# ScalarE's first activation is an exponential of one zero, issued before the first rows of q and k arrive

## The chip, the cores and the metric

The kernel runs on one core of one Trainium2 chip. The metric is the device time of one execution in microseconds, the median of several runs. Five engines work side by side, each on its own stream of instructions in order: PE (TensorE), DVE (VectorE), ACT (ScalarE), POOL (GpSimd) and SP (SyncE, which here only issues DMAs). They wait for one another through semaphores.

## What is computed

Windowed attention with sink tokens, then a two-layer feed-forward network with a gate h * sigmoid(h), all in float32:

```python
scores = (1/sqrt(D)) * q @ k.T                     # B=4, H=8, S=768, D=64
keep   = is_sink | in_window                       # n_sink=4, window=128: integers given at run time
a      = softmax(where(keep, scores, -1e9))
x      = (a @ v) laid out as (3072, 512)
h      = x @ w_in                                  # 512 x 2048
out    = (h / (1 + exp(-h))) @ w_out               # 2048 x 512
```

The two weights arrive as 64-bit numbers and are turned into float32 on the chip.

## The kernel before

**Tiles and stages.** The 3072 rows are eight chunks of 384 (index c). Each chunk has four pairs of heads, so there are 32 pairs p. Pairs 0 to 7 (chunks 0 and 1) take a path of their own, the functions whose names begin with f_: q and k are transposed by PE against the identity matrix (f_prep, L667), scores are made per head j of the pair (f_scores, L699), the exponential and the division by its sum follow (f_softmax, L737), the probabilities are transposed (f_ptrans, L757) and multiplied with v (f_av, L778). Pairs 8 to 31 take other functions (q_prep, k_prep, v_prep, scores, softmax, ptrans, strans, av). For every chunk, 16 column blocks of h are then made by mlp1 (L843, names h), gated by act (L857, names gh and gl) and multiplied with w_out by mlp2 (L869, names out).

**The weights** come in 32 pieces of 512 KB in four groups (weight, L808): SP loads a piece into the tile wraw, of which there are two buffers, three DVE instructions build the float32 bits in wcv (L41, L42, L43), ACT makes the high part (L826: winh or wouth) and POOL or DVE the low part (L828). A third piece can be loaded only when the L43 of the first is done.

**The masks.** Their limits are the two run-time integers. ACT issues two small DMAs into the tile words (L211), DVE turns them into limits (L215 to L220) and builds the masks m0, m1, m2 and mf (L250 to L276), in order and ahead of everything else that it does. The first instruction of the attention on DVE is L688, which puts the sink keys behind a block of keys kT; the third score matmul of a head reads them. L727 then adds a mask to the scores and takes the row minimum of the negated sum, which the exponential of ACT at L742 uses.

**ACT's first data work** is the copy of transposed q (qlf or qdf, L687) and of transposed k (kT, L684) out of PSUM. ACT holds one table of functions at a time, and an ACT_TABLE_LOAD is placed by the compiler before the first activation that needs another table. In the kernel before the first one stands in front of the first L687 copy, and the copies and the exponentials L742 after it need no other. The gate (Silu, L863 and L864) needs another table, and so the loads alternate later.

**What sets the order.** The program calls the pieces in an order of due times (the table OPT, L928 to L998), and the framework's scheduler then gives each engine its stream: it goes by its own estimates of durations, so a change of one instruction can move others far away. Tiles in pools with one or two buffers make a DMA wait until the last reader of the old contents is done; SP is in order, and a DMA that waits holds everything behind it.

The lines at the head of the program are these:

```python
    ident = const.tile([P, P], F32, name="ident")          # L203
    make_identity(nc, ident)
    warm = OPT["warm"]                                      # L206
    words = const.tile([P, 4], I32, name="words")
    for i, src in enumerate((n_sink, window)):
        nc.scalar.dma_start(words[:, 2 * i : 2 * i + 2], src.bitcast(I32).partition_broadcast(P))   # L211
```

Of the kernel before, what the change touches and what calls it, by code (L numbers as in the profile page):

```python
# [8 lines left out]
F32 = mybir.dt.float32  # L9
F32R = mybir.dt.float32r  # L10
I32 = mybir.dt.int32
AF = mybir.ActivationFunctionType
# [157 lines left out]
def attn_moe_kernel(  # L170
# [11 lines left out]
    nc = tc.nc  # L182
# [19 lines left out]
    const = ctx.enter_context(tc.tile_pool(name="const", bufs=1))  # L202
    ident = const.tile([P, P], F32, name="ident")  # L203
    make_identity(nc, ident)

    warm = OPT["warm"]  # L206

# [827 lines left out]
```

## Time and profile before

| what | value |
|---|---|
| three runs | 722.54, 724.70, 723.37 us |
| their median | 723.37 us |
| the profiled execution's own time | 723.66 us |
| its span in the trace | 721.8 us |
| granted clock of PE over the span | 0.998 |
| PE busy | 705.0 us, 3842 matmuls |
| ACT busy | 489.4 us |
| DVE busy | 481.3 us |
| POOL busy | 281.5 us |
| bytes moved | 61.86 MB |

The profiled execution's time is 1.86 us above its span. A row of the trace gives the start in microseconds from the span's start, the busy time, the engine, the line, the operation, out<-in, and in brackets the idle time ahead of it with what ended it. SPq and ACTq are DMA issues by SP and ACT; the landing of a DMA has no row of its own, and is seen where an engine waits for it. A row with a count above 1 merges instructions of one line.

### The profile page before, as it was taken

How to read it: one execution, taken by the hardware profiler on the slowest of the kernel's cores; microseconds unless marked ns; L12 is line 12 of the kernel's file. 1: busy time of each engine (PE TensorE's matmuls, PEld its weight loads, DVE VectorE, ACT ScalarE, POOL GpSimd, SP SyncE). 2: the span in 40 equal slices, each digit the busy share in tenths (PEclk: the TensorE clock that was granted, in tenths of full speed). 3: DMA queues.
4: the chain of work that ended last, by engine and by line, in shares of the span. 5: the costliest groups of instructions: out<-in, count | busy, mean ns of one | idle time of the engine just before them, and what ended most of it. 6: DMA issues, size and time to landing. Idle time of an engine off the chain costs nothing.

```text
span 721.8 us, 12275 instructions
## 1 busy us (share of the span) xinstructions
PE 705.0 (98%) x3842; PEld 624.1 (86%) x3842; DVE 481.3 (67%) x1323; ACT 489.4 (68%) x1165; POOL 281.5 (39%) x667
## 2 busy tenths in 40 slices
PE   6998999999999999999999999999999999999997
PEld 4676778798999999999999999999999999998986
DVE  5899767976776687667866777767866776731111
ACT  4889788786776777777666777777667876732112
POOL 3310000055655666444555455544554554430000
PEclk9999999999999999999999999999999999999999
DMA  7556546434522262114521353114412321001001
GB/s 180 176 154 186 148 112 173 151 84 107 147 43 40 70 187 63 22 39 138 138 41 27 84 166 66 35 34 120 136 27 41 106 58 35 1 1 45 0 1 46
DMA packets 141334, 61.86 MB, mean 86 GB/s; under 512 B 130001, under 2 KB 130001, under 8 KB 141265
## 3 DMA queue, kind: packets, MB, share of 16 engines
q1 hardware_dynamic: 140976, 61.04, 32.9%
q8 instruction: 31, 0.51, 0.3%
q14 instruction: 39, 0.31, 0.1%
q10 hardware_dynamic: 288, 0.00, 0.0%
HBM read 54.72 MB, written 6.29 MB: 85 GB/s over the span
## 4 chain that ended last, share of the span: by engine, by line
PE 81%; DMA 5%; DVE 5%; ACT 3%; POOL 2%; issue 2%; SPq 1%; DVEq 0%; POOLq 0%; ACTq 0%
PE h L852 32%; PE out L880 11%; PE out L879 11%; PE out L878 11%; PE o L575 4%; DMA wraw<-in_moe_w_in_dram 3%; PE o L788 2%; PE s L468 2%; PE s L464 2%; PE pt L520 2%; DMA wraw<-in_moe_w_out_dram 2%; PE o L591 1%; DVE wcv L43 1%; DVE wcv L42 1%; PE o L584 1%
## 5 line engine op out<-in xcount | busy, mean ns | idle before, releaser
L852 PE MATMUL h<-xh,winh 128*128 128x384 f32 x512 | 177.2, 346 | 0.0
L852 PE MATMUL h<-xh,winl 128*128 128x384 f32 x512 | 173.9, 340 | 0.0
L852 PE MATMUL h<-xl,winh 128*128 128x384 f32 x512 | 172.7, 337 | 0.0
L878 PE MATMUL out<-wouth,gh 128*128 128x512 f32 x384 | 153.2, 401 | 1.7 <-ACT gh L863 1.6
L879 PE MATMUL out<-woutl,gh 128*128 128x512 f32 x384 | 151.8, 396 | 0.5 <-DVE woutl L828 0.3
L880 PE MATMUL out<-wouth,gl 128*128 128x512 f32 x384 | 150.2, 396 | 0.0
L863 ACT ACTIVATE gh<-h 128x384 fp32r<-128x384 f32 x128 | 62.9, 492 | 104.4 <-PE h L852 100.7
L866 DVE TENSOR_TENSOR gl<-sg,gh 128x384 fp32r<-128x384 f32 x128 | 75.4, 589 | 87.2 <-ACT sg L864 84.9
L852 PEld LDWEIGHTS h<-xh,winh 128*128 128x128 f32 x512 | 96.3, 188 | 3.0 <-issue 0.9
L852 PEld LDWEIGHTS h<-xl,winh 128*128 128x128 f32 x512 | 96.5, 189 | 2.1
L852 PEld LDWEIGHTS h<-xh,winl 128*128 128x128 f32 x512 | 96.2, 188 | 0.5 <-issue 0.3
L880 PEld LDWEIGHTS out<-wouth,gl 128*128 128x128 f32 x384 | 71.8, 188 | 17.2 <-DVE gl L866 0.6
L878 PEld LDWEIGHTS out<-wouth,gh 128*128 128x128 f32 x384 | 72.2, 188 | 14.4 <-ACT gh L863 2.4
L879 PEld LDWEIGHTS out<-woutl,gh 128*128 128x128 f32 x384 | 72.1, 188 | 13.2 <-DVE woutl L828 1.3
L505 POOL TENSOR_SCALAR pm<-pm,r 128x128 f32<-128x128 f32 x144 | 61.5, 442 | 42.5 <-DVE r L490 39.2
L485 ACT ACTIVATE pm<-pm,mx 128x264 f32<-128x264 f32 (+1 forms) x144 | 70.6, 492 | 1.3 <-DVE mx L472 0.3
L440 POOL TENSOR_TENSOR vs<-vn,vs 128x256 fp32r<-128x256 f32 (+1 forms) x48 | 33.3, 695 | 91.4 <-ACT vs L438 78.2
L864 ACT ACTIVATE sg<-h 128x384 f32<-128x384 f32 x128 | 62.5, 488 | 0.5
L472 DVE CUSTOM_DVE_ANT_0 pm<-s,m 128x264 f32<-128x264 f32 (+1 forms) x144 | 52.9, 411 | 11.9 <-PE s L468 11.6
L600 DVE TENSOR_TENSOR x<-o,x 64x512 f32<-64x512 f32 x48 | 32.8, 683 | 35.5 <-ACT x L599 34.4
L419 POOL CAST ks<-ksA 128x24 fp32r<-128x24 f32 (+1 forms) x24 | 4.8, 201 | 131.7 <-PE s L468 73.0
L438 ACT CAST vs<-vn 128x256 fp32r<-128x256 f32 (+1 forms) x48 | 18.6, 388 | 50.1 <-PE o L584 49.6
(162 smaller groups left out, 1337.7 us busy)
## 6 DMA issues: line engine op xcount, KB each, us to landing
wraw<-in_moe_w_in_dram SPq DMA_DIRECT2D x16, 512.0 KB
wraw<-in_moe_w_out_dram SPq DMA_DIRECT2D x16, 512.0 KB
wchk<-in_moe_w_in_dram SPq DMA_DIRECT2D x16, 512.0 KB
wchk<-in_moe_w_out_dram SPq DMA_DIRECT2D x16, 512.0 KB
qn<-in_q_dram SPq DMA_DIRECT2D x96, 48.0 KB
kn<-in_k_dram SPq DMA_DIRECT2D x64, 64.0 KB
vn<-in_v_dram SPq DMA_DIRECT2D x32, 128.0 KB
out_dram<-ost SPq DMA_DIRECT2D x7, 512.0 KB
```

Of the source, the lines that this page charges most:

```text
L440: nc.gpsimd.tensor_tensor(vs[:, j0:, j, 1, :], vn[:, j0:, j, :], vs[:, j0:, j, 0, :], ALU.subtract)
L472: nc.vector.tensor_tensor_reduce(out=pm[:, t, off:], in0=sp[:, :w], in1=(m0, m1, m2)[min(blk, 2)], scale=-0.125, scalar=3.0e38, op0=ALU.ad ...
L485: nc.scalar.activation(x, x, AF.Exp, bias=mx[:, p, j * NTB + t : j * NTB + t + 1], scale=-1.0, accum_out=r[:, t : t + 1],)
L505: nc.gpsimd.tensor_scalar(x, x, r[:, t : t + 1], 1.0, ALU.mult, ALU.mult)
L600: nc.vector.tensor_tensor(x32[:, :n], o[0:64, :n], x32[:, :n], ALU.add)
L852: nc.tensor.matmul(hps[:, :CT], w[g][:, cc, fs], s[x], start=n == 0, stop=n == 3 * NCC - 1)
L863: nc.scalar.activation(gh, hps[:, :CT], AF.Silu)
L864: nc.scalar.activation(sg, hps[:, :CT], AF.Silu)
L866: eng.tensor_tensor(gl, sg, gh, ALU.subtract)
L878: nc.tensor.matmul(o, gh[:, ts_], wout_h[g][:, f], start=fc == 0, stop=False)
L879: nc.tensor.matmul(o, gh[:, ts_], wout_l[g][:, f], start=False, stop=False)
L880: nc.tensor.matmul(o, gl[:, ts_], wout_h[g][:, f], start=False, stop=fc == NFC - 1)
```

## The change

A tile of one element is set to zero by DVE, and ACT takes its exponential, in the program ahead of the two small DMAs of the limits. Nothing reads the result.

```diff
     ident = const.tile([P, P], F32, name="ident")
     make_identity(nc, ident)
 
+
+    early = const.tile([1, 1], F32, name="early")
+    nc.vector.memset(early, 0.0)
+    nc.scalar.activation(early, early, AF.Exp)
+
     warm = OPT["warm"]
```

Behind this place every line number of the changed kernel is 5 higher (L687 becomes L692). Numbers at the end of a tile's name are buffer numbers; they are 3 higher in the changed kernel.

**The start of ACT's stream.** Before:

```order
L211 DMA words<-in_n_sink_dram 128x2
L211 DMA words<-in_window_dram 128x2
L687 ACT_TABLE_LOAD
L687 COPY qlf<-qt_173 64x384
L684 COPY kT_181<-kt_174 128x3x128
```

and now:

```order
L216 DMA words<-in_n_sink_dram 128x2
L209 ACT_TABLE_LOAD
L209 ACTIVATE early<-early 1x1
L216 DMA words<-in_window_dram 128x2
L692 COPY qlf<-qt_176 64x384
L689 COPY kT_184<-kt_177 128x3x128
```

The first table load moves from the first copy to the place between the two small DMAs, and the new activation stands behind it. The number of table loads is the same in both streams, 67 (64 of them run in the trace of before; the others stand in a path for other inputs).

**DVE from the third weight piece on** (pairs 0 and 1 of the heads). Before:

```order
L42 SCALAR_TENSOR_TENSOR wcv_2_398<-wraw_2_396,wcv_2_398 128x512
L746 TENSOR_SCALAR r_0_293<-r_0_293 128x3
L43 SCALAR_TENSOR_TENSOR wcv_2_398<-wraw_2_396,wcv_2_398 128x512
L688 COPY kT_280<-kt_273 128x8
L747 RECIPROCAL r_0_293<-r_0_293 128x3
L774 COPY pTz_151<-pb_1_303 128x384
L772 COPY pTz_151<-pa_0_302 8x128
L727 ISA pm_1_0_316,mx<-s_1_0_319,m_94 128x128
```

and now:

```order
L751 TENSOR_SCALAR r_0_296<-r_0_296 128x3
L42 SCALAR_TENSOR_TENSOR wcv_2_401<-wraw_2_399,wcv_2_401 128x512
L752 RECIPROCAL r_0_296<-r_0_296 128x3
L693 COPY kT_283<-kt_276 128x8
L779 COPY pTz_154<-pb_1_306 128x384
L732 ISA pm_1_0_319,mx<-s_1_0_322,m_97 128x128
...
L732 ISA pm_1_2_321,mx<-s_1_2_323,m_99 128x264
L732 ISA mx 128x1
L777 COPY pTz_154<-pa_0_305 8x128
L43 SCALAR_TENSOR_TENSOR wcv_2_401<-wraw_2_399,wcv_2_401 128x512
```

The small copy of transposed probabilities (L772, now L777) has moved behind the three score instructions of the next head, and the third step of the weight piece (L43) behind both. On ACT, at the same place, the three multiplications by the reciprocal (L753, now L758) have moved ahead of the copy L771 (now L776) that the small copy waits for.

**SP around the fifth weight piece.** Before:

```order
L802 DMA wraw_3_443<-in_moe_w_in_dram 128x1024
L642 DMA qn_543<-in_q_dram 128x3x64 x2
L642 DMA kn_544<-in_k_dram 128x3x64
L805 DMA wraw_4_486<-in_moe_w_out_dram 128x1024
L654 DMA vn_313<-in_v_dram 128x3x64 x2
L642 DMA kn_544<-in_k_dram 128x3x64
```

and now:

```order
L807 DMA wraw_3_446<-in_moe_w_in_dram 128x1024
L387 DMA vsn<-in_v_dram 8x4x64
L647 DMA qn_546<-in_q_dram 128x3x64 x2
L647 DMA kn_547<-in_k_dram 128x3x64 x2
L659 DMA vn_316<-in_v_dram 128x3x64 x2
L810 DMA wraw_4_489<-in_moe_w_out_dram 128x1024
```

The fifth weight piece, wraw_4, has moved behind the two loads of vn, into whose buffer pair 0's second product with v must first have been read out.

**ACT at the first gate** (names gh_0 and sg_0). Before:

```order
L753 ACTIVATE pm_0_637<-pm_0_637,r_0_688 128x264
L863 ACT_TABLE_LOAD
L863 ACTIVATE gh_0_698<-h_0_675 128x384
L864 ACTIVATE sg_0_697<-h_0_675 128x384
L826 CAST winh_135<-wcv_2_669 128x512
```

and now:

```order
L868 ACT_TABLE_LOAD
L868 ACTIVATE gh_0_701<-h_0_678 128x384
L758 ACTIVATE pm_0_640<-pm_0_640,r_0_691 128x128
L758 ACTIVATE pm_0_640<-pm_0_640,r_0_691 128x256
L758 ACTIVATE pm_0_640<-pm_0_640,r_0_691 128x264
L831 CAST winh_138<-wcv_2_672 128x512
L869 ACTIVATE sg_0_700<-h_0_678 128x384
```

The load and the first gate have moved ahead of the three multiplications, and the second use of the gate behind them. The streams differ at many more places up to about the 600th of PE's 3944 rows, and PE's order is the same behind that.

## Rows read from the trace of the kernel before

**Rows 1.** The page's head: the span, the busy time of PE, and PE's busy share in 40 equal slices of the span, in tenths.

```profile
span 721.8 us, 12275 instructions
PE 705.0 (98%) x3842; PEld 624.1 (86%) x3842; DVE 481.3 (67%) x1323; ACT 489.4 (68%) x1165; POOL 281.5 (39%) x667
PE   6998999999999999999999999999999999999997
```

**Rows 2.** Stretches of the span (us): its length, then busy us of PE, PEld (weight loads), DVE, ACT and POOL with the number of instructions, PE's granted clock, share of the DMA engines, GB/s.

```profile
0.00:10.00 10.00, 5.91 (x24) 4.55 (x24) 4.61 (x23) 2.60 (x4) 4.12 (x15) 0.93 0.67 142
40.00:50.00 10.00, 10.00 (x55) 6.95 (x54) 8.59 (x26) 8.01 (x23) 1.28 (x1) 1.00 0.60 175
60.00:70.00 10.00, 8.91 (x46) 7.01 (x45) 8.94 (x20) 9.93 (x24) 0.00 (x0) 1.00 0.49 156
200.00:300.00 100.00, 100.00 (x566) 91.92 (x566) 73.12 (x192) 72.29 (x171) 57.14 (x129) 1.00 0.32 76
```

**Rows 3.** ACT in order of time from the span's start: the second of its two DMA issues, the first table load and the first two copies.

```profile
1.35 0.45 ACTq L211 DMA_DIRECT2D words<-in_window_dram  x1
6.20 1.28 ACT L687 ACT_TABLE_LOAD   x1 [6.20 <-PE qt L673]
7.49 0.47 ACT L687 COPY qlf<-qt 64x384 f32<-64x384 f32 x1
7.87 0.47 ACT L684 COPY kT<-kt 128x384 f32<-128x384 f32 x1
```

**Rows 4.** DVE in order of time: its first instruction, the first that reads the limits, the copy of the sink keys, the first mask on scores, and the first step on the second weight piece.

```profile
0.97 0.06 DVE L920 MEMSET one<- 128x1 f32 x1 [0.97 <-PEq L1019]
5.10 0.17 DVE L215 CAST wf<-words 128x4 f32<-128x4 int32 x1 [4.07 <-DMA words<-in_window_dram]
9.83 0.16 DVE L688 COPY kT<-kt 128x8 f32<-128x8 f32 x1
10.08 0.29 DVE L727 CUSTOM_DVE_ANT_0 pm<-s,m 128x128 f32<-128x128 f32 x1
13.23 0.43 DVE L41 TENSOR_SCALAR wcv<-wraw 128x512 int32<-128x512 int32 x1 [0.99 <-DMA wraw<-in_moe_w_in_dram]
```

**Rows 5.** PE and its weight loads in order of time: the first score matmuls, and the weight load of the first third score.

```profile
8.48 2.81 PE L720 MATMUL s<-kT,qlf 128*128 128x128 f32 x6 [1.49 <-ACT kT L684]
10.04 0.50 PEld L720 LDWEIGHTS s<-kT,qlf 128*128 128x128 f32 x2 [0.72 <-DVE kT L688]
```

**Rows 6.** PE in order of time from 20 to 80 us: all rows ahead of which it idled.

```profile
24.18 1.51 PE L788 MATMUL o<-pTz,vn 128*64 128x384 f32 x6 [0.27 <-DVE pTz L772]
28.51 1.51 PE L788 MATMUL o<-pTz,vn 128*64 128x384 f32 x6 [0.46 <-DVE pTz L772]
36.67 1.51 PE L788 MATMUL o<-pTz,vn 128*64 128x384 f32 x6 [0.60 <-DVE pTz L772]
55.77 0.33 PE L765 MATMUL pa<-ident,pm 128*128 128x128 f32 x1 [0.61 <-ACT pm L753]
58.38 0.50 PE L878 MATMUL out<-wouth,gh 128*128 128x512 f32 x1 [0.46 <-ACT gh L863]
64.38 0.50 PE L878 MATMUL out<-wouth,gh 128*128 128x512 f32 x1 [1.09 <-ACT gh L863]
78.89 0.92 PE L720 MATMUL s<-kT,qdf 128*128 128x128 f32 x4 [0.48 <-ACT pTz L776]
```

**Rows 7.** ACT and DVE in order of time around pair 0's second head and pair 1: the copy and the three multiplications on ACT; on DVE the copies of transposed probabilities and the first score instruction of the next head.

```profile
23.23 0.37 ACT L771 COPY pTz<-pa 128x256 f32<-128x256 f32 x1
24.02 1.21 ACT L753 ACTIVATE pm<-pm,r 128x128 f32<-128x128 f32 x3
...
23.41 0.53 DVE L774 COPY pTz<-pb 128x384 f32<-128x384 f32 x1
23.86 0.27 DVE L772 COPY pTz<-pa 8x128 f32<-8x128 f32 x1
24.06 0.27 DVE L727 CUSTOM_DVE_ANT_0 pm<-s,m 128x128 f32<-128x128 f32 x1
24.96 0.07 DVE L727 DVE_READ_ACCUMULATOR2_ANT mx<- 128x1 f32 x1
```

**Rows 8.** SP in order of time: the issue of wraw_4 and of pair 2's vn.

```profile
24.29 0.42 SPq L805 DMA_DIRECT2D wraw<-in_moe_w_out_dram  x1
25.72 0.90 SPq L654 DMA_DIRECT2D vn<-in_v_dram  x2
```

**Rows 9.** DVE and ACT in order of time: the first step on wraw_4, the third step on wraw_3, the reciprocal of pair 2's first head, and the multiplications that read it.

```profile
29.33 0.41 DVE L41 TENSOR_SCALAR wcv<-wraw 128x512 int32<-128x512 int32 x1
29.67 0.69 DVE L43 SCALAR_TENSOR_TENSOR wcv<-wraw,wcv 128x512 int32<-128x512 int32 x1
31.67 0.17 DVE L747 RECIPROCAL r<-r 128x3 f32<-128x3 f32 x1
32.69 1.21 ACT L753 ACTIVATE pm<-pm,r 128x128 f32<-128x128 f32 x3
```

**Rows 10.** The chain of work that ended last: from the start of a weight piece's issue to its landing (start, us, what).

```profile
8.02 5.19 DMA wraw<-in_moe_w_in_dram
58.30 3.53 DMA wraw<-in_moe_w_out_dram
70.79 4.36 DMA wraw<-in_moe_w_in_dram
```

## The prediction

> **What bounds the kernel now.** I read the page's head first, then PE by stretches, then the start of each engine in order of time. PE is busy 705.0 of 721.8 us [rows 1], and from 200 to 300 us all of the time [rows 2]. There nothing but the count and size of the matmuls sets the time, and the change touches no matmul. What it can move is the lead-in, where PE idles: 10.00 - 5.91 = 4.1 us in the first 10 us [rows 2], and 0.27 + 0.46 + 0.60 + 0.61 + 0.46 + 1.09 + 0.48 = 3.97 us from 20 to 80 us [rows 6]. PE waits there for DVE and ACT. From 40 to 50 us it has no idle time [rows 2], so that what is late before 40 us is still late behind 50.
>
> A measurement of this kernel can tell 0.3% from no change: 2.2 us of 723.37.
>
> **The table load.** In the kernel before, the first load runs from 6.20 to 7.48 us, 1.28 us, and holds the first copies: q at 7.49, k at 7.87 to 8.34 [rows 3]. PE waits for that copy of k for 1.49 us and makes the first scores at 8.48 [rows 5]. With the load done before, the copies could begin near 6.2, about 1.3 us sooner. I cost this gain at nothing, for this reason: DVE is late as well. It gets the limits at 5.10, builds masks without a gap that matters up to 9.83, copies the sink keys then and puts the first mask on scores at 10.08 [rows 4]. The third score of the head waits for those sink keys: its weight load stands at 10.04, after 0.72 us of waiting for DVE's L688 [rows 5]. So scores that are ready a microsecond sooner wait for DVE until the same 10.08. The cover is the masks; if it were gone, the gain would be at most 1.29 us, the time from 6.20 to 7.49.
>
> **What is added.** One memset of one element on DVE, where a like one takes 0.06 us at 0.97, with 4.07 us of idle time behind it [rows 4]: nothing. One activation of one element on ACT. No row has this shape; the smallest nearby is no larger than the 0.47 us of a copy [rows 3], and ACT does nothing else up to 6.20: nothing.
>
> **The DMA that is moved past.** The table load now stands between ACT's two small DMAs. The second brings the window, and DVE's first mask instruction waits for it up to 5.10 [rows 4]. It was issued at 1.35 [rows 3]. Two bounds: if its issue doesn't wait for the engine, it is later by next to nothing; if it stands behind the whole load and the activation, by 1.28 + 0.47 = 1.75 us, and the mask chain with it. Of that, 0.99 us would be taken up where DVE waits for the second weight piece at 13.23 [rows 4], and 0.76 us remain. The trace of before has no DMA of ACT behind an activation, so no row decides. The DMA doesn't depend on the activation and no semaphore of it stands between them, so I take the lower value, 0, and keep 0.76 as a rival. [...]
>
> [...] The row shows that the copy begins 0.01 us after the load's 1.28 us end [rows 3]. [...]
>
> **The new order.** The scheduler has rearranged the streams from some 21 us on. I follow three places.
>
> *First, the copies of transposed probabilities.* In the kernel before, ACT makes its copy at 23.23, DVE its small one at 23.86 to 24.13, and PE's product with v starts at 24.18 [rows 6, 7]. Now three multiplications, 1.21 us, stand ahead of ACT's copy, which would run from 24.44 to 24.81. On DVE the three score instructions stand ahead of the small copy; they took from 24.06 to 25.03, 0.97 us [rows 7], and would run from 23.86 to 24.83. So the small copy ends at 24.83 + 0.27 = 25.10 and the product starts at 25.15, 0.97 us late. At 28.51 PE waited 0.46 us for DVE [rows 6]; if DVE itself is not later there, 0.51 us remain. Bounds: 0, since the multiplications come sooner and the next transposes want them, and 0.97.
>
> *Second, wraw_4.* The load of vn waits for the end of that product: 25.69, and it is issued at 25.72 [rows 6, 8]. wraw_4 was issued ahead of it, at 24.29 [rows 8], and now stands behind it: 25.72 + 0.97 + 0.90 for the two issues of vn + 0.05 to the next = 27.64, 3.35 us later. A weight piece lands 3.53 to 5.19 us after its issue; I take the middle row, 4.36 [rows 10], so 32.0. DVE came to its first step on it at 29.33; with wraw_3's third step, 0.69 us, now ahead of it, and 0.51 us late, it comes at 30.53 [rows 9]. It waits for 1.47 us, in order, and the reciprocal of pair 2 stands behind. In the kernel before that reciprocal ended 2.51 us after 29.33, at 31.84 [rows 9]; two steps of 0.69 us have left the stretch, so 1.13 us now, and it ends at 30.53 + 1.47 + 1.13 = 33.13. The multiplications that read it started at 32.69 [rows 9], with 0.51 us of lateness 33.20. So the wait is just covered: 0. With 5.19 us of landing it ends at 33.96 and costs 0.76 us more; with 3.53, nothing.
>
> *Third, the first gate.* The load and the gate go ahead of multiplications of 1.2 us. PE's waits at 55.77 and 58.38, 0.61 and 0.46 us, are for these very rows [rows 6]. But ACT is busy for 9.93 of the 10 us from 60 to 70 [rows 2], and between the first and the second gate it has the same rows to work off in either order. What PE gains at 55 to 58 us it waits at 64.38, where it already waits 1.09 us for the second gate [rows 6]. I take 0, with a bound of 1.07 us of gain.
>
> **The sum.** 0 for the load, 0 for what is added, 0 for the moved DMA, 0.51 for the first place, 0 for the second, 0 for the third. The profiled execution took 723.66 us, so 724.2; it lies 0.29 us above the median of the three runs, and against that median the forecast is 723.37 + 0.51 = **723.9 us**: no difference that can be measured. I give it 0.48.
>
> **Rivals.**
>
> *The window's DMA is held behind the load.* For it: the issue stands behind them in an in-order stream. Against it: nothing makes it wait. 723.9 + 0.76 = 724.6 us, still within 0.3%. Chance 0.18. [...]
>
> *The weight stream stays late, slower.* wraw_4's 3.35 us are handed on: there are two buffers, so each piece can be issued only when the piece two before it is worked off, and a late one makes all behind it late. For it: the landings of weight pieces at 58.30 and 70.79 stand on the chain that ended last [rows 10], and DVE's steps on the pieces stand in order ahead of what PE waits for. Against it: PE ran from 40 to 50 us without idling, so some pieces were in time. It decides from the point at which DVE waits for wraw_4 longer than the 1.47 us above, and later pieces of the stream, too, find it waiting. 723.9 + 3.35 = 727.2 us. Chance 0.22.
>
> *The waits for ACT go, faster.* With the gate first, the waits at 55.77, 58.38, 64.38 and 78.89 vanish: 0.61 + 0.46 + 1.09 + 0.48 = 2.64 us [rows 6], and the lateness of the first place is taken up. 723.37 - 2.64 = 720.7 us. For it: all four are waits for ACT, whose order has changed there. Against it: ACT is full and gets no work less. Chance 0.12.
>
> **The numbers.** Faster by over 0.3% is the last rival alone, 0.12. Within 0.3% are the forecast and the held DMA, 0.48 + 0.18 = 0.66. Slower is the weight stream, 0.22. The range goes from 721.2, at the edge of the faster rival, of which most is left out, to 727.2, the price of the slower one, whose upper half is left out: together about 0.2.
>
> **What would show it.** Right: the load near 1.3 us and no other before the first gate; the window's DMA within 0.3 us of 1.35 and DVE's first mask instruction near 5.1; the first mask on scores near 10.1 as before, though the copies of q and k end a microsecond sooner; the product at 24.18 later by about 1 us; wraw_4 issued near 27.6; PE's idle time from 20 to 80 us between 3 and 6 us. Wrong: DVE's first mask instruction near 6.9 (the held DMA); PE idle by over 6 us from 20 to 80 us, with waits that end on weight pieces; or scores that go on at 9 us, which would mean that the masks were not the cover.

## The result, and the profile after

The changed kernel takes 727.62 us (median of 8 runs, 726.04 to 729.57) against 723.76 us of the kernel before (8 runs beside it): a ratio of 1.0052, 95% interval 1.0038 to 1.0067. It is slower by half a per cent, 3.9 us. The forecast was 723.9 us and no difference; the upper end of its range, 727.2, is passed too. The profiled execution took 727.98 us, 1.7 us more than its span.

The page's head of the changed kernel, as in [rows 1]:

```profile
span 726.3 us, 12276 instructions
PE 708.0 (97%) x3842; PEld 626.5 (86%) x3842; DVE 480.9 (66%) x1324; ACT 490.1 (67%) x1166; POOL 284.4 (39%) x667
PE   7897999999999999999999999999999999999997
```

The span is 4.5 us longer, but PE's busy time only 3.0 us, with the same 3842 matmuls. From the fifth slice on both rows read alike. Stretches as in [rows 2], and the one ahead of the gates:

```profile
40.00:50.00 10.00, 10.00 (x58) 7.70 (x57) 8.43 (x24) 7.15 (x22) 2.57 (x2) 1.00 0.60 174
50.00:60.00 10.00, 7.36 (x38) 4.73 (x36) 8.07 (x24) 7.51 (x19) 0.00 (x0) 1.00 0.84 212
60.00:70.00 10.00, 8.87 (x39) 7.61 (x39) 8.65 (x24) 9.93 (x22) 0.00 (x0) 0.83 0.61 174
200.00:300.00 100.00, 100.00 (x566) 91.77 (x565) 72.58 (x184) 71.08 (x165) 61.00 (x135) 1.00 0.31 74
```

PE idles for 2.6 us between 50 and 60, and from 60 to 70 its granted clock is 0.83 where it was 1.00. The start of ACT, as in [rows 3]:

```profile
1.35 1.28 ACT L209 ACT_TABLE_LOAD   x1 [1.35 <-PEq L1024]
1.42 0.40 ACTq L216 DMA_DIRECT2D words<-in_window_dram  x1
2.65 0.20 ACT L209 ACTIVATE early<-early 1x1 f32<-1x1 f32 x1
6.42 0.47 ACT L692 COPY qlf<-qt 64x384 f32<-64x384 f32 x1 [3.57 <-PE qt L678]
7.03 0.48 ACT L689 COPY kT<-kt 128x384 f32<-128x384 f32 x1
10.17 0.40 ACT L747 ACTIVATE pm<-pm,mx 128x128 f32<-128x128 f32 x1 [2.16 <-DVE mx L732]
```

The load has moved to 1.35. The window's DMA is issued at 1.42, inside the load, so the load doesn't hold it. The copies come a microsecond sooner, and then ACT waits 2.16 us for DVE. DVE and PE in the same stretch, as in [rows 4, 5]:

```profile
5.04 0.17 DVE L220 CAST wf<-words 128x4 f32<-128x4 int32 x1 [3.97 <-DMA words<-in_window_dram]
9.77 0.16 DVE L693 COPY kT<-kt 128x8 f32<-128x8 f32 x1
9.85 0.28 DVE L732 CUSTOM_DVE_ANT_0 pm<-s,m 128x128 f32<-128x128 f32 x1
7.66 1.62 PE L725 MATMUL s<-kT,qlf 128*128 128x128 f32 x4 [0.66 <-ACT kT L689]
9.98 1.25 PE L725 MATMUL s<-kT,qlf 128*128 128x264 f32 x2 [0.71 <-DVE kT L693]
```

PE makes its first scores 0.82 us sooner; the sink keys and the first mask are sooner by 0.06 and 0.23 us only. The masks are the cover. Now all rows from 20 to 84 us ahead of which PE idled, as in [rows 6]:

```profile
25.54 1.51 PE L793 MATMUL o<-pTz,vn 128*64 128x384 f32 x6 [1.29 <-DVE pTz L777]
33.80 1.51 PE L793 MATMUL o<-pTz,vn 128*64 128x384 f32 x6 [0.40 <-DVE pTz L777]
38.35 1.51 PE L793 MATMUL o<-pTz,vn 128*64 128x384 f32 x6 [1.13 <-DVE pTz L777]
56.10 0.52 PE L678 MATMUL qt<-ident,qn 128*128 128x128 f32 x3 [1.00 <-DMA qn<-in_q_dram]
61.13 0.50 PE L883 MATMUL out<-wouth,gh 128*128 128x512 f32 x1 [2.74 <-ACT gh L868]
83.18 0.92 PE L725 MATMUL s<-kT,qdf 128*128 128x128 f32 x4 [0.41 <-ACT pTz L781]
```

They sum to 6.97 us against 3.97 [rows 6]. The product at 38.35 waits longer, a wait for q's rows is new, and three waits at the gates (0.61, 0.46, 1.09) have become one of 2.74. The chain of work that ended last, as this execution's profile has it (start, us, what):

```profile
25.21 0.29 DVE pTz L777
25.54 1.52 PE o L793 x6
...
28.07 3.71 DMA wraw<-in_moe_w_out_dram
31.80 0.43 DVE wcv L41
...
33.80 1.52 PE o L793 x6
...
38.35 1.51 PE o L793 x6
```

Read alone, it says that the late product holds wraw_4's issue up to 28.07, that the landing of wraw_4 (3.71 us) holds DVE, and that the products at 33.80 and 38.35 are late by that. The runs below show otherwise: with wraw_4 asked for ahead of vn again, both products wait as long as here (sp_old, first_weights_old). A chain shows what ended last in one execution, not what would be gained if a link were taken out.

### The profile page after: what moved, and what is told of

It is laid out like the page before. It is cut to its first block, busy times and chain, and to the rows that moved or that the text cites. A ratio compares the mean times of both kernels' runs of the same rounds, so it can differ in the third digit from the quotient of the medians.

```text
span 726.3 us, 12276 instructions
## 1 busy us (share of the span) xinstructions
PE 708.0 (97%) x3842; PEld 626.5 (86%) x3842; DVE 480.9 (66%) x1324; ACT 490.1 (67%) x1166; POOL 284.4 (39%) x667
## 4 chain that ended last, share of the span: by engine, by line
PE 85%; DMA 4%; ACT 3%; POOL 2%; DVE 2%; SPq 2%; issue 1%; DVEq 0%; POOLq 0%; ACTq 0%
PE h L857 33%; PE out L885 11%; PE out L884 11%; PE out L883 11%; PE o L580 4%; PE o L793 3%; PE s L469 2%; PE s L473 2%; DMA wraw<-in_moe_w_in_dram 2%; PE pt L525 2%; PE s L725 1%; PE o L596 1%; DMA qn<-in_q_dram 1%; PE o L589 1%; DMA wchk<-in_moe_w_in_dram 1%
## 5 line engine op out<-in xcount | busy, mean ns | idle before, releaser
L510 POOL TENSOR_SCALAR pm<-pm,r 128x128 f32<-128x128 f32 x144 | 63.2, 456 | 40.4 <-DVE r L495 38.7
L541 POOL TENSOR_SCALAR_AFFINE_SELECT pq<-pq 128x384 fp32r<-128x384 f32 (+1 forms) x96 | 50.6, 527 | 6.6 <-ACT pq L534 4.8
```

What stands on the lines that cost most here:

```text
L510: nc.gpsimd.tensor_scalar(x, x, r[:, t : t + 1], 1.0, ALU.mult, ALU.mult)
L541: nc.gpsimd.affine_select(out=before, in_=own, pattern=[[0, n], [-1, P]], compare_op=ALU.is_gt, fill=0.0, base=0, channel_multiplier=1,)
```

## Experiments

To separate the exponential from the order of the streams, each experiment writes every engine's order out as a table and fixes it with edges that keep an engine's instructions in that order and wait for nothing. "Old" is the order of the kernel before, "new" that of the changed one; a place is an instruction's number on its engine. The table stands at the head of these kernels, so their line numbers are higher than those of the changed kernel; tiles keep their names.

```diff
+    for e, by in ORDER.items():
+        by = [int(x) for x in by.split()]
+        row = traced[e]
+        row = [row[n + by[n]] if n < len(by) else row[n] for n in range(len(row))]
...
+        for a, b in zip(row, row[1:]):
+            tc.add_manual_dep(b, a.name, mybir.DependencyInfo(
+                mybir.DependencyClass.NoSync, mybir.DependencyReason.DATA), reason="order")
```

All results, each against the kernel before on the same chip:

| kernel | what is in the new order | median us (runs) | ratio, 95% interval |
|---|---|---|---|
| the change | all | 727.62 (8) | 1.0038 to 1.0067 |
| early_old_order | nothing | 723.51 (12) | 0.9989 to 1.0006 |
| late_new_order | all, no early exponential | 728.02 (6) | 1.0048 to 1.0075 |
| new_order_first | up to 48 us | 726.42 (6) | 1.0027 to 1.0051 |
| new_order_later | from 48 us on | 726.09 (12) | 1.0019 to 1.0040 |
| gate_place_old | all but the gates | 727.40 (5) | 1.0035 to 1.0062 |
| gate_place_new | the gates | 724.23 (11) | 1.0000 to 1.0018 |
| first_weights_old | up to 48 us, SP old | 725.75 (7) | 1.0016 to 1.0039 |
| sp_old | all but SP | 727.35 (5) | 1.0032 to 1.0060 |
| first_place_old | all but the first product's place | 726.87 (5) | 1.0037 to 1.0065 |
| third_step_old | all but one weight step's place | 726.88 (5) | 1.0030 to 1.0058 |
| three_places_old | all but first place, weight step, gates | 726.71 (5) | 1.0025 to 1.0052 |
| cover_old | all but the place ahead of the gates | 728.22 (6) | 1.0039 to 1.0068 |
| cover_new | the place ahead of the gates | 724.95 (11) | 1.0009 to 1.0027 |
| second_place_old | all but 28 to 48 us | 726.78 (5) | 1.0026 to 1.0054 |
| tail_new | from 66 us on | 724.61 (11) | 0.9999 to 1.0017 |
| wait_filled | all, the gate's wait filled | 726.29 (5) | 1.0026 to 1.0053 |
| cover_old_filled | cover_old, the wait filled | 726.47 (5) | 1.0021 to 1.0047 |
| products_old_filled | all but both late products, filled | 725.33 (12) | 1.0010 to 1.0033 |

The intervals are some 2 us wide, so a difference of about 1 us between two of these rows is no more than a hint.

**Exponential or order.** Theory A was that the order costs the time, A1 ahead of 48 us, A2 behind it; the rival was the early load itself.

```diff
 # early_old_order: the changed kernel, all streams in the old order
+    early = const.tile([1, 1], F32, name="early")
+    e1 = nc.vector.memset(early, 0.0).ins
+    e2 = nc.scalar.activation(early, early, AF.Exp).ins
 # late_new_order: the kernel before, all streams in the new order
-    nc.vector.memset(early, 0.0)
-    nc.scalar.activation(early, early, AF.Exp)
```

> The exponential of one zero stands first as in the changed kernel, and every other instruction of every engine is held in the order that the kernel before has. Theory A (the loss of 3.9 us comes from the order that the scheduler made anew, not from the load): 723.0 to 724.0 us, no loss, and at most some tenths of gain. Theory B (the early load or the activation itself costs, by what it does to the start): 726.5 to 728.5 us. If the earlier copies are worth their 1.3 us: 722.5 us.

Measured 723.51 us. The early load by itself costs nothing and gains nothing that shows: by the interval at most 0.8 us gained, less than the 1.29 us of earlier copies, and at most 0.4 us lost.

> No early exponential: the first table load stands in front of the first copy of q as in the kernel before, and every instruction of every engine is held in the order of the changed kernel. Theory A (the order costs): 727 to 728.5 us. Theory B (the early load costs): 723 to 724 us. Between the two, 725 to 726 us, if both have a share.

Measured 728.02 us. The order alone is the whole loss.

```diff
 # new_order_first: early exponential; places below PE 126, DVE 105, ACT 70, SP 40 new, the others old
 # new_order_later: early exponential; those places old, the others new
```

> Early exponential; the changed kernel's order up to about 48 us (PE's first 126, DVE's 105, ACT's 70 and SP's 40 instructions), and from there on the order of the kernel before. Theory A1 (the loss is laid in the first 48 us: the product with v is late, the fifth weight piece waits behind the loads of vn, the q of the sixth pair comes late behind the weight pieces, and PE idles until its clock falls): 726.5 to 728.5 us. Theory A2 (the loss is laid by the order of the gates and weight pieces behind 48 us): 723.5 to 725 us.

> Early exponential; the order of the kernel before up to about 48 us and the changed kernel's order from there on. Theory A1 (loss in the first 48 us): 723 to 724.5 us. Theory A2 (loss behind 48 us): 726.5 to 728.5 us.

Measured 726.42 and 726.09 us, 2.5 and 2.2 us above the kernel before: each stretch costs by itself (by the intervals 2.0 to 3.7 and 1.4 to 2.9 us), and neither the whole. Both A1 and A2 are half right.

**The gates and SP's order.** Next the candidates were the gates' order (A), the weight pieces' order on SP (B) and the late product (C).

```diff
 # gate_place_old: these places of PE old (gate_place_new: these new, all others old); also ACT's and DVE's beside them
-L883 MATMUL out<-wouth,gh_0   x3, with L884 x3
 L770 MATMUL pa_4<-ident,pm_4  and L771 to L775
 ...
+L883 MATMUL out<-wouth,gh_0   x3, with L884 x3
 # first_weights_old, sp_old: SP's stream
-L659 DMA vn<-in_v_dram x2
 L810 DMA wraw_4<-in_moe_w_out_dram
+L659 DMA vn<-in_v_dram x2
```

> The changed kernel with its early exponential and its own order, but with the old kernel's order at one place: the first two gates of the feed-forward part (PE's places 174 to 216, VectorE's 121 to 151, ScalarE's 83 to 104). Theory A, the gate place: putting the products with gh_0 ahead of the transposes of pair 4 made one wait of 2.74 us of three that summed to 2.16 us, and the slower matmuls behind it cost another us or so; with the old order there the waits are again about .6, .5 and 1.1 us, and the time falls by 1.5 to 2.2 us below the changed kernel's 727.6, to 725.4 to 726.1 us. Theory B, the weight stream: the loss comes along SP's queue, whose order is untouched, and the time stays at 727.6 us, within 0.5. Theory C, the product with v: most is lost ahead of 48 us, and the time is 726.4 us or more, with less than 1.2 us won.

> The early exponential, the old kernel's order everywhere, and the new order only at the first two gates (PE's places 174 to 216, VectorE's 121 to 151, ScalarE's 83 to 104). Theory A: the 2.74 us wait appears, and the time is that of the kernel with the new order from 48 us on, 726.1 us, within 0.7. Theory B: with the weight stream as before, ScalarE reaches gh_0 earlier and the wait is under 2 us; the time is 723.5 to 724.3 us. If the cost of that later stretch lies in reorderings behind the gates, the time is 723.5 us too, but with the 2.74 us wait in the profile.

Measured 727.40 and 724.23 us: the place counts for 0.2 us out of the changed order and 0.4 us alone, and theory A's 1.5 to 2.2 fell, though the wait of 2.74 us appears and goes with it.

> The early exponential, the new order up to about 48 us on TensorE, VectorE and ScalarE, the old order afterwards, and the old order on SP throughout, so that the weight piece wraw_4 is asked for ahead of v's rows again. The kernel that had the new order on SP too took 726.4 us. Theory B (the lateness of that stretch is carried by the weight pieces): 723.5 to 724.3 us, and the products with v catch up by 48 us. Theory C (it is the order on the three engines, the product with v waiting for ScalarE's copy): 726 us or more, with the products with v late by .8 to 1.3 us.

> The changed kernel with its early exponential and its own order on TensorE, VectorE, ScalarE and GpSimd, and with the old kernel's order on SP alone. Theory B: 723.5 to 725 us, most of the loss gone, and q's rows of pair 5 land before TensorE asks for them. Theories A and C: 727 to 728 us, as the changed kernel.

Measured 725.75 and 727.35 us. With wraw_4 ahead of vn again most of the loss stays: 1.9 us of 2.5 in the first kernel, a little less than theory C expected, and nearly all in the second. B fell as a matter of SP's order. The profile of sp_old says why; SP, DVE and PE in order of time:

```profile
26.77 0.34 SPq L926 DMA_DIRECT2D wraw<-in_moe_w_out_dram  x1
34.10 0.28 DVE L893 COPY pTz<-pa 8x128 f32<-8x128 f32 x1 [0.30 <-ACT pTz L892]
34.43 1.51 PE L909 MATMUL o<-pTz,vn 128*64 128x384 f32 x6 [0.37 <-DVE pTz L893]
38.98 1.51 PE L909 MATMUL o<-pTz,vn 128*64 128x384 f32 x6 [1.13 <-DVE pTz L893]
```

wraw_4 is asked for early, and DVE's first step on it (32.04) waits for no DMA. The two products wait 0.37 and 1.13 us all the same, as in the changed kernel (0.40 and 1.13): the small copy of the first now waits for ACT.

**Single places.** What was left were the first product's place, VectorE's third step on the seventh weight piece, and the granted clock.

```diff
 # first_place_old: ACT (and DVE's and PE's places beside it)
+L776 COPY pTz<-pa_1
 L758 ACTIVATE pm<-pm,r x3
-L776 COPY pTz<-pa_1
 # third_step_old: DVE
+L43 SCALAR_TENSOR_TENSOR wcv_6<-wraw_6,wcv_6
 L801 TENSOR_TENSOR xl<-o,xh
 L779 COPY pTz<-pb_3
 L751 TENSOR_SCALAR r<-r
-L43 SCALAR_TENSOR_TENSOR wcv_6<-wraw_6,wcv_6
 # three_places_old: both, and gate_place_old's
```

> The changed kernel with its early exponential and its own order, but with the old order at the first place alone: ScalarE's places 23 to 38, VectorE's 46 to 64 and two of TensorE's, so that the probabilities' copies to pTz stand ahead of the three multiplications and of the next masks again. Theory C (the wait of TensorE for these copies, 1.29 us against .28, is handed on to the end): the first wait falls to about .3 us and the time to 726.0 to 726.7 us. Theory D (TensorE catches up later anyway, because q's rows of pair 5 or the gates end last): 727.2 us or more.

Measured 726.87 us, 0.75 less than the changed kernel: a gain just short of theory C's and above D's, and within the scatter of the runs. In its profile the first wait is 0.27 us.

> The changed kernel with its early exponential and its own order, but with the old order at six of VectorE's places, 98 to 103, so that the third step (L43) of weight piece 6 no longer stands behind the division's first step, which waits for ScalarE's exponentials. Theory D (late conversion holds the buffer of the next weight piece, and this piece's transfer runs beside q's rows of pair 5, for which TensorE waits 1.00 us): the next piece is asked for at 44.5 to 45.5 us instead of 46.82, the wait for q's rows falls under .4 us, and the time falls by .6 to 1.2 us, to 726.4 to 727.0 us. Theory C: no more than .4 us.

Measured 726.88 us, within theory D's range, but not for its reason. SP and PE of this kernel:

```profile
44.95 4.13 SPq L923 DMA_DIRECT2D wraw<-in_moe_w_in_dram  x2
55.74 0.52 PE L794 MATMUL qt<-ident,qn 128*128 128x128 f32 x3 [0.82 <-DMA qn<-in_q_dram]
```

The next weight piece is asked for 1.87 us sooner, as expected, and the wait for q's rows is still 0.82 us. Theory D fell.

> The changed kernel with its early exponential, the new order everywhere but at three places, which are in the old order together: the first place, the third step of weight piece 6, and the first two gates. If the three carry the loss: 723.5 to 724.8 us, within .3% of the kernel before. If the loss is spread over the other reorderings too: 725.0 to 726.5 us. If none of the three counts while others give waits: 727 us or more.

Measured 726.71 us, between the ranges for "spread" and for "none of the three counts": with all three places old 3 us are still lost, so most of the loss lies elsewhere.

**The place ahead of the gates, the second product, the rest.**

```diff
 # cover_old: PE (cover_new: this place alone new)
-L857 MATMUL h_1<-xh_1,winh and three more
 L793 MATMUL o3<-pTz,vn x3
 L678 MATMUL qt4<-ident,qn4 x3, kt4 x3
+L857 MATMUL h_1<-xh_1,winh and three more
 # second_place_old: PE 100 to 126, DVE 64 to 105, ACT 38 to 70, SP 28 to 40 old
 # tail_new: up to PE 216, DVE 151, ACT 104, SP 60 old, new behind
```

> The changed kernel with its early exponential and its own order, but with the old order at the place ahead of the gates alone (PE's places 130 to 174, ScalarE's 70 to 83, VectorE's 105 to 121): the four products h0_1 stand behind the transposes of pair 4 again, between the transposes that free q's buffer and those that need q's next rows. Theory F (these products were the cover of that load): the wait of 1.00 us for q's rows falls under .5 us and the time by .6 to 1.2 us, to 726.4 to 727.0 us. Theory G (the load lands late for another reason, and the wait stays or moves): 727.2 us or more.

> The early exponential, the old order everywhere, and the new order only at the place ahead of the gates (PE's places 130 to 174, ScalarE's 70 to 83, VectorE's 105 to 121). Theory F: a wait for q's rows of pair 5 of .3 to 1.0 us appears, and the time is 723.8 to 724.8 us. Theory G: no such wait, 723.5 us, as with the old order.

Alone the place costs 1.2 us (724.95), just over what F expected; its profile shows a wait for q's rows of 0.16 us only. Taken out, it gains nothing: 728.22 us, the slowest median of all, with 0.55 us of that wait left. F is not shown.

> The changed kernel with its early exponential and its own order, but with the old order from about 28 to 48 us (PE's places 100 to 126, VectorE's 64 to 105, ScalarE's 38 to 70, SP's 28 to 40), which holds the second late product with v (TensorE's wait of 1.13 us against .60) and the weight pieces' order on SP. If the second product counts by its wait: .5 us less, 726.9 to 727.2 us; if the weight stream of that stretch counts too: 726.0 to 726.8 us; if neither: 727.4 us or more.

Measured 726.78 us, 0.84 less; the wait at the second product is 0.61 us again.

> The early exponential, the old order up to about 66 us on all engines, and the new order behind it. If the loss is made ahead of 66 us: 723.2 to 723.9 us. If the reorderings behind it cost too: 724.3 us or more, and the lateness in the profile grows behind 66 us.

Measured 724.61 us, 0.85 above the kernel before, with an interval that just includes 1. In the profile the lateness doesn't grow behind 66 us (0.44 us at the first gate, 0.25 at the twentieth), so this remains undecided.

**The clock.** In the changed kernel PE waits 2.74 us for gh_0, up to 61.13. Its windows there (columns as in [rows 2]):

```profile
58.00:60.00 2.00, 0.38 (x2) 0.00 (x0) 1.56 (x7) 1.96 (x5) 0.00 (x0) 1.00 0.85 193
60.00:62.00 2.00, 0.87 (x3) 0.73 (x4) 1.96 (x7) 1.99 (x5) 0.00 (x0) 0.95 0.68 194
62.00:64.00 2.00, 2.00 (x8) 1.49 (x7) 1.29 (x3) 1.98 (x4) 0.00 (x0) 0.50 0.66 190
64.00:66.00 2.00, 2.00 (x11) 1.95 (x10) 1.93 (x5) 1.99 (x8) 0.00 (x0) 0.70 0.41 125
```

Behind 2.74 us of idleness the clock falls to 0.50, and from 62 to 64 PE is fully busy with 8 matmuls. Ten matmuls that nobody reads fill the wait:

```diff
 # wait_filled: the changed kernel; mlp2, chunk 0, first block, ahead of the products with gh_0
+                for n in range(10):
+                    i = nc.tensor.matmul(
+                        mst["o", 0], st[0]["xh"][:, :P], wout_h[0][:, 0], start=True, stop=True
+                    ).ins
```

> The changed kernel with its early exponential and its own order, and with ten matmuls more that nobody reads (wouth with xh, into the bank that the products with gh_0 start afresh), which fill 2.35 us of TensorE's wait of 2.74 us ahead of these products. Theory E (the granted clock falls behind that wait, and the slower matmuls cost about 1.1 us): the clock stays at 1.00 from 58 to 70 us in the profile, gh_1 is late by about 2.7 us instead of 3.85, and the time falls by .5 to 1.1 us, to 726.5 to 727.1 us. If the clock falls for another reason, or in few executions: 727.3 to 727.9 us.

Measured 726.29 us, 1.33 less than the changed kernel and a little below theory E's range. The runs of the two overlap (725.89 to 727.22 against 726.04 to 729.57), so the gain is not clear of their scatter. PE of this kernel in order of time:

```profile
57.59 2.70 PE L998 MATMUL out<-wouth,xh 128*128 128x512 f32 x10
60.70 0.50 PE L1005 MATMUL out<-wouth,gh 128*128 128x512 f32 x1 [0.41 <-ACT gh L984]
```

and the window in which the changed kernel is slow:

```profile
62.00:64.00 2.00, 2.00 (x15) 1.84 (x14) 1.68 (x4) 1.97 (x4) 0.00 (x0) 1.00 0.87 269
```

The clock stays at 1.00, and PE gets through 15 matmuls in this window. The expectation was wrong in one point: gh_1 is late by 3.43 us here too, since from gh_0 to gh_1 the lateness against the kernel before grows by 1.10 us in both kernels: ACT sets gh_1, and its three multiplications now stand between the two gates.

What brings the fall, and what it costs, shows when all profiled executions are set side by side. The lateness is the start of a gate's first product less its start in the kernel before.

| profiled executions | PE waits for gh_0, for gh_1 (us) | PE's clock from 58 to 70 us | lateness gained from the first to the third gate |
|---|---|---|---|
| gate_place_old, three_places_old, new_order_first, first_weights_old, early_old_order, cover_new, tail_new (old order at the gates) | 0.46, 1.09 or 1.10 | 1.00 | 0.00 us, within 0.01 |
| wait_filled, cover_old_filled, products_old_filled | 0.41, 1.32 or 1.33 | 1.00 | 1.55 us |
| third_step_old, new_order_later | 2.75, 2.74; 1.33 | 1.00 | 1.55, 1.54 us |
| the change, late_new_order, first_place_old, second_place_old, sp_old | 2.74 or 2.75, none | 0.50 for some 3.4 us | 1.76 to 1.79 us |
| cover_old, gate_place_new | 2.74, none | 0.50 for some 6.8 us (gate_place_new: means of 0.86 from 50 to 60 and 0.80 from 60 to 70) | 3.00, 2.85 us |

The clock falls in the wait for gh_0 or just behind it in seven of the nine executions that have the unfilled wait, and in none of the others, the kernel before included. Where it doesn't fall, PE waits 1.33 us for gh_1; where it falls, PE is too slow to wait there. Counted from gh_0's first product, the scores ahead of gh_1 start 1.59 us later in the changed kernel (67.68) than in third_step_old (65.73), and the first product with gh_1 starts with no difference: the slow stretch has used up the wait. What is left at the third gate is 1.79 - 1.55 = 0.24 us, and it comes by way of DVE, whose mask waits for the late scores and holds gl_1 behind it:

```profile
68.54 0.29 DVE L732 CUSTOM_DVE_ANT_0 pm<-s,m 128x128 f32<-128x128 f32 x1 [0.53 <-PE s L725]
```

In cover_old, slow for twice as long, 3.00 - 1.55 = 1.45 us are left.

The gain of 1.33 us is therefore not shown to be the clock's. From gh_0 to the twentieth gate the lateness grows by 1.61 us in the changed kernel and by 0.40 with the wait filled. Of these 1.21 us, 0.24 stand at the third gate and 0.48 at the twelfth, and 0.70 come between the twelfth and the thirteenth, where the changed kernel waits 0.59 us for a weight piece's low part (133.83) and wait_filled does not. new_order_later waits there too (0.61 us at 132.23) and grows by 1.59 us, with a clock of 1.00 throughout.

The clearest test is the slowest kernel, in which the clock stays down longer. cover_old's windows:

```profile
58.00:60.00 2.00, 0.00 (x0) 0.00 (x0) 1.84 (x6) 1.98 (x3) 0.00 (x0) 0.99 0.85 218
60.00:62.00 2.00, 1.33 (x3) 1.14 (x4) 1.51 (x7) 1.99 (x6) 0.00 (x0) 0.50 0.58 156
62.00:64.00 2.00, 2.00 (x7) 1.42 (x7) 1.71 (x4) 1.97 (x4) 0.00 (x0) 0.50 0.88 271
64.00:66.00 2.00, 2.00 (x10) 2.00 (x9) 1.97 (x5) 1.98 (x8) 0.00 (x0) 0.50 0.18 44
```

```diff
 # cover_old_filled: cover_old with wait_filled's ten matmuls
 # products_old_filled: first_place_old and second_place_old with them
```

> The kernel cover_old (728.2 us; its profile showed TensorE's clock at .50 from 60 to 66 us, behind the wait of 2.74 us for gh_0), with ten matmuls more that nobody reads, which fill that wait. Theory E (the clock falls because of the wait): 1.00 from 58 to 70 us in the profile and 726.0 to 727.2 us, a gain of 1.0 to 2.2 us. If the clock has nothing to do with the wait: 727.7 us or more, or a clock that falls all the same.

Measured 726.47 us, 1.75 less, as expected; five of cover_old's six runs lie above all five of this kernel's. Its window:

```profile
62.00:64.00 2.00, 2.00 (x15) 1.89 (x14) 1.96 (x4) 1.97 (x4) 0.00 (x0) 1.00 0.89 287
```

The lateness from gh_0 to the twentieth gate grows by 2.86 us in cover_old and by 1.13 with the wait filled: 1.73 us, as the medians have it, and 1.45 of them stand at the third gate already. Here profile, runs and medians agree: the clock's cost is shown, by this one pair.

> The changed kernel with its early exponential and new order, with the two places of the late products (24 and 38 us) and the weight pieces' order between in the old order, and with the ten matmuls that fill the wait for gh_0. One at a time these gave .75, .85 and 1.3 us. If they add up: 724.4 to 725.1 us. If they overlap, because a later wait takes up what an earlier one gives: 725.5 to 726.3 us.

Measured 725.33 us, between the two ranges and 2.29 less than the changed kernel, and the two intervals don't overlap; the three gains one at a time sum to 0.75 + 0.84 + 1.33 = 2.92. The kernel has the old order up to 48 us but for a few of SP's places, so it is nearly new_order_later with the wait filled, and is 0.76 us below it. 1.2 to 1.6 us of loss remain (ratio 1.0022). None of these kernels beats the kernel before by more than a measurement can tell.

## Why the prediction was wrong, step by step

**Right, with its sizes.** *The table load gains nothing*: the masks cover it, and early_old_order shows it by itself. *What is added* costs nothing: the activation takes 0.20 us. *The window's DMA is not held*: issued at 1.42 inside the load, DVE's first mask instruction at 5.04. No row of before decided this 0; the changed kernel's trace does. The activation starts 0.02 us after the load's end (2.63, 2.65). ACT was idle ahead of this load, but a later load between busy activations, from 63.08 to 64.36, is followed as closely (64.38).

**The first place, right.** The small copy was put at 24.83 and is at 25.21, the product at 25.15 and is at 25.54; of its lateness 0.51 us was to remain, and at the third product 0.82 - 0.34 = 0.48 does. (0.34 us is how late the first product is in this execution, which late_new_order has at 0.04.) Taken out, it is worth 0.75 us in the medians, within the scatter of the runs.

**The second place, right in its times, wrong in what makes PE wait.** SP, DVE and ACT, as in [rows 8, 9]:

```profile
27.08 0.90 SPq L659 DMA_DIRECT2D vn<-in_v_dram  x2
28.07 3.77 SPq L810 DMA_DIRECT2D wraw<-in_moe_w_out_dram  x2
31.80 0.43 DVE L41 TENSOR_SCALAR wcv<-wraw 128x512 int32<-128x512 int32 x1 [0.33 <-DMA wraw<-in_moe_w_out_dram]
32.95 0.17 DVE L752 RECIPROCAL r<-r 128x3 f32<-128x3 f32 x1
33.31 0.80 ACT L758 ACTIVATE pm<-pm,r 128x128 f32<-128x128 f32 x2
```

wraw_4 was put at 27.64 and is issued at 28.07, the reciprocal's end at 33.13 and is 33.12, the multiplications at 33.20 and are at 33.31. DVE waits 0.33 us for the piece instead of the 1.47 forecast. So far the 0 holds, but the forecast followed the weight piece and the reciprocal alone. PE waits 0.40 us at 33.80, where it had no wait, and 1.13 instead of 0.60 at 38.35, 0.93 us more in all, and with the piece early it still does (sp_old). For the second of these the rows of ACT give the reason, first of the kernel before, then of the changed one:

```profile
34.19 0.48 ACT L795 CAST xh<-o 128x384 fp32r<-128x384 f32 x1 [0.29 <-PE o L788]
35.95 0.35 ACT L771 COPY pTz<-pa 128x256 f32<-128x256 f32 x1
36.20 0.62 ACT L826 CAST wouth<-wcv 128x512 fp32r<-128x512 f32 x1
...
35.35 0.48 ACT L800 CAST xh<-o 128x384 fp32r<-128x384 f32 x1 [0.83 <-PE o L793]
35.72 0.62 ACT L831 CAST winh<-wcv 128x512 fp32r<-128x512 f32 x1
37.63 0.35 ACT L776 COPY pTz<-pa 128x256 f32<-128x256 f32 x1
```

The cast of a weight piece stood behind the copy of the probabilities and now stands ahead of it, between xh and the three exponentials: from xh to the copy it is 2.28 us instead of 1.76, and the 0.52 are PE's longer wait. With the old order of this stretch the wait is 0.61 again and the time 0.84 us less (second_place_old), a gain within the scatter.

**The third place, wrong in its reason, small in its size.** "I take 0" rested on ACT having the same work in either order, and ACT does pay back between the first and the second gate what it won ahead of the first. But PE's order had changed there as well: its transposes of pair 4 and a score now stand behind the products with gh_0. Nothing covers PE from 58.4 to 61.1, one wait of 2.74 us stands for three of 2.16 in sum, and the clock, for which the forecast had no term, falls behind it. In the changed kernel's profile that costs 0.24 us. With the old order here the time is 0.2 us less (gate_place_old), and with the new order here alone 0.4 us more (gate_place_new).

**The step that failed is the sum.** It gave 0.51 us for the whole new order: three places priced, two of them at 0, and nothing, without a reason, for all the others. The runs show 2.5 us for the order up to 48 us alone (new_order_first), where the sum had 0.51, and 2.2 us for the order from there on (new_order_later), where it had 0. Up to 48 us the profile has the first place as forecast, and 0.93 us more of waiting at the second. Behind 48 us it has a wait of 1.00 us for q's rows, never followed, and 0.58 us more at the gates. Of the places put in the new order alone, all else old, only the one ahead of the gates, never followed either, is clear of the noise: 1.2 us (cover_new). No run takes the loss apart to the end.

**The slower rival** had nearly the price (727.2 us) and not the mechanism. The weight pieces from the fifth to the twelfth are issued 1.1 to 7.3 us late, but from 20 to 84 us PE waits for none of them (at 133.83 it waits 0.59 us for a piece's low part, and the kernel before 0.19 and 0.32 us near there); SP's old order brings nothing (727.35), and an earlier piece does not shorten the wait for q's rows. That its price came near the measured time is chance. The prediction's sign of this rival, PE idle by over 6 us from 20 to 80 us, came half: 6.56 us, and no wait ends on a weight piece. **The faster rival** and the held DMA did not come.

**The sum, redone** on the profiled execution: waits of PE 6.97 - 3.97 = 3.00 us and a late start of 0.34 make 3.34 of the 4.5 us by which the spans differ. The slow stretch takes another 1.59 us of PE's time, against third_step_old. That makes 4.93, 0.4 us too much, and no run shows where it is won back. Of the 3.00 us the wait for q's rows, 1.00, has no cause that a run settles. It varies between executions: the same order has 1.00 us in the changed kernel's profile and none in wait_filled's. Also open is why cover_new alone costs 1.2 us while its profile, the quickest of its runs, has the waits of the old order and 0.16 us more, and whether the order behind 66 us counts.

## What to carry to other kernels

A change that is free by itself can move a whole schedule: take the new streams as the change, go through every place at which an engine in the lead-in waits, on the waiting engine's own stream too, and give the places that were not followed a cost of their own. A single long wait of TensorE can cost more than its length: with one of 2.74 us the clock fell to 0.50 in seven of nine executions, and in none with waits of 0.46 and about 1.1 us at this place. But the slow stretch cost only what was left of it when the next wait was used up (0.24 us in the changed kernel and 1.45 in cover_old). Before a link of the critical chain is called the cause, take it out. To find out whether a change or its side effects cost the time, fix the order of the streams and exchange one without the other.

## What was not expected of the hardware

TensorE's granted clock fell to 0.50 after one idle stretch of 2.74 us, though the engine had been busy without a gap from 40 to 50 us; by the windows' means it stayed there some 3.4 us in the changed kernel and 6.8 in cover_old, and in two of nine executions with this wait it didn't fall. The window's DMA was issued at 1.42 us in the changed kernel, 0.07 us after the table load had started on the same engine and 1.21 ahead of its end. The same 96 KB of pair 5's q rows were there 6.82 us after the transposes that free their buffer had begun in first_weights_old's profile (49.18 to 56.00) and in under 5.19 us in wait_filled's (50.48 to 55.67, without a wait).
